# Cosformer attention and a mixture of adapters: the order of numerators, transposition and copy in a slot, q turned further ahead, rows of k retimed

## The chip, the cores and the metric

The kernel runs on one core of a Trainium2 chip. The metric is the device time of one execution in microseconds. Engines are named as in the profile: PE is TensorE, PEld its weight loads, DVE is VectorE, ACT is ScalarE, POOL is GpSimd, SP is SyncE.

## What is computed

Eight batches of eight heads, 576 tokens, head width 64. A linear attention with cosine and sine weights feeds a mixture of eight low-rank adapters, of which each token takes two.

```python
r = np.maximum(x, 0.0)                       # phi, for q and for k
phi = np.concatenate([r * cos_w, r * sin_w], axis=-1)
kv = np.einsum('bhsf,bhsd->bhfd', k_p, v)
z = np.sum(k_p, axis=2)
num = np.einsum('bhsf,bhfd->bhsd', q_p, kv)
den = np.einsum('bhsf,bhf->bhs', q_p, z)[..., None] + 1e-06
x = (num / den)                              # as (4608, 512): token by 8 heads of 64
logits = x @ w_gate                          # 8 adapters, the two largest are kept
w = softmax of the two kept logits
out = x + sum over the two of w * ((x @ A[e]) @ B[e])      # rank 16
```

## The kernel before

The 4608 tokens are 36 tiles of 128. Tiles 0 to 3 are tokens of batch 0, tile 4 holds 64 tokens of batch 0 and 64 of batch 1 (a mixed tile), tiles 5 to 8 are batch 1, tiles 9 to 12 batch 2, 13 is mixed, and so on: two batches take nine tiles, and batch b first appears in tile b // 2 * 9 + b % 2 * 4. The products of k and v of a batch (72 small matmuls, `kv`, in nine rows s of eight) must be done, and copied to SBUF by `kv_out`, before the batch's first tile has its numerators.

The body is one written-out loop over slots n = 0 to 34, one for each tile but the last. `tc.manual_schedule()` leaves each engine's instructions in the order in which the code issues them, so the text of the loop is the order of each engine's queue. What a tile goes through:

- `move_q(n)`: TensorE multiplies q with diagonal matrices of cosines and sines (`transp_q`, line 213, and 201 from tile 27 on), which turns q and weights it; ScalarE empties the two PSUM buffers with a relu (`evac_q`, line 229).
- `numden(n)`: numerators and denominators, eight products into the PSUM tile `nd`, of which there is one (line 257). The epsilon is added by two small products (line 252), or, where `eps_dve(n)` holds (n over 13 and slot n has rows of k), by VectorE (line 268).
- `normalise(n)`: VectorE takes the reciprocal (line 270) and multiplies (line 277) out of `nd` into `xt`.
- `transp_x(n)`: four transpositions on TensorE into `xz` (line 285); `evac_x(n)`, VectorE's copy to `xT` (line 291), which in every third slot takes along the transposed gates of a group (`transp_z`, line 359).
- `logits(n)`: four products (line 311) with the adapters' A and the gate weights. Three tiles form a group.
- `gate_a(g)`, `gate_sig(g)`, `gate_b(g)`: the two largest logits (lines 320 to 328, VectorE), a sigmoid (ScalarE, line 337), and the weighting (lines 344 and 346, VectorE) in the slot after.
- `delta`, `delta_add`, `evac_o`, `store`: the output product or products, ScalarE's copy, for late tiles GpSimd's addition of x, and the DMA to memory. Stores are held back until the loads are through.

k of a batch is turned into its weighted rows by several engines: VectorE clears the negatives of the rows that GpSimd takes (`relu_k`, line 165), GpSimd multiplies these with cosine and sine (`scale_k1`, line 156), VectorE and ScalarE take some rows whole (lines 153 and 151). In which slot, the tables `relu_at`, `pool_at`, `act_at`, `dve_at` and `kv_at` say; they are filled for b = 2 to 7 from `at`, `n_pool` and the batch's first tile. Behind GpSimd's rows of batch b its queue issues the loads of k of b + 3, q of b + 2 and v of b + 3. The gates stand in slots 6, 8, 10, 12, 15, 18, 21, 24, 27, 30 and 33 (`gate_a_at`); from slot 12 on the last logits of the group stand in the same slot, ahead of the gate.

The order of one slot before, on the engines that matter: copy of x of tile n - 1 (DVE), `normalise(n)` (DVE), `move_q(n + 1)` (PE, ACT), rows of k (PE), logits (PE), gates (DVE), output products (PE), `transp_x(n)` and `transp_z` (PE), rows of k (DVE, POOL), `numden(n + 1)` (PE).

Of the kernel before, what the change touches and what calls it, by code (L numbers as in the profile page):

```python
# [13 lines left out]
NS = 9  # L14
# [5 lines left out]
def kernel(ctx, tc, q, k, v, w_gate, A, Bw, out):  # L20
    nc = tc.nc
    B, H, S, D = q.shape
# [8 lines left out]
    NT = B * NS // 2  # L31
# [1 line left out]

    persist = ctx.enter_context(tc.tile_pool(name="persist", bufs=1))
    p_kp = ctx.enter_context(tc.tile_pool(name="p_kp", bufs=3))
    p_qpt = ctx.enter_context(tc.tile_pool(name="p_qpt", bufs=6))
    p_kv = ctx.enter_context(tc.tile_pool(name="p_kv", bufs=3))
    p_x = ctx.enter_context(tc.tile_pool(name="p_x", bufs=14))
    p_xt = ctx.enter_context(tc.tile_pool(name="p_xt", bufs=7))
# [24 lines left out]
    def load_k(b, eng=None):  # L64
        load(eng or nc.gpsimd, k_b[b].rearrange("p g s d -> p g (s d)"), k, b)

    def load_q(b):
        load(nc.gpsimd, q_b[b].rearrange("p g s d -> p g (s d)"), q, b)

    def load_v(b):  # L70
        load(nc.gpsimd, v_b[b][:, 0:VN].rearrange("p (g x) -> p g x", g=G), v, b)
# [161 lines left out]
    def move_q(n):  # L233
        transp_q(n)
        evac_q(n, 0)
        evac_q(n, 1)
# [58 lines left out]
    groups = [list(range(i, i + 3)) for i in range(0, NT - 3, 3)]  # L295
# [130 lines left out]
    def put(at, step, what):  # L426
        at.setdefault(step, []).append(what)
# [5 lines left out]
    kv_at[3] = [(1, s) for s in (5, 4, 7, 8, 6)]  # L433
    for b in range(2, B):
        first = b // 2 * NS + b % 2 * 4
        at = {2: 5, 3: 8, 4: 12, 5: 17, 6: 20, 7: 23}[b]
        n_pool = {2: 5, 3: 7, 4: 8, 5: 8}.get(b, 9)
        for s0, s1 in ((0, 3), (3, n_pool)):
            put(relu_at, at, (b, s0, s1))
        for s in range(n_pool):  # L440
            put(pool_at, at, (b, s))
        for i in range(2):
            if n_pool <= 7:
                put(dve_at, at, (b, 7, i))
            if n_pool < 9:
                put(act_at, first - 4 + i, (b, 8, i))
            if n_pool == 5:
                put(act_at, first - 3 + i, (b, 6, i))
                put(act_at, first - 2, (b, 5, i))
        order = (7, 0, 1, 2, 3, 4, 8, 6, 5) if n_pool <= 7 else (0, 1, 2, 3, 4, 5, 8, 6, 7)  # L450
        if n_pool == 9:
            order = range(NS)
        for j, s in enumerate(order):

            if b == 2:
                ahead = 2 if j < 4 else 1
            elif b == 3:
                ahead = 3 if j < 2 else 2 if j < 5 else 1
            else:
                ahead = 4 - min(j // 2, 3)  # L460
            put(kv_at, first - ahead, (b, s))

# [15 lines left out]
    with tc.manual_schedule():  # L480
# [17 lines left out]
        load_q(2)  # L498
        load_k(3)
        load_v(3)  # L500
        load_k(4)
        load_q(3)
        load_v(4)
        kv_out(0)
        transp_q(0)
        evac_q(0, 0, "dve")
        evac_q(0, 1)
        numden(0)

        g10, g11, g12 = range(len(groups) - 3, len(groups))  # L510
        todo, held = [], []
# [11 lines left out]
                held.append(d)  # L523

        for n in range(NT - 1):
            if n > 0:
                g = move_at.get(n - 1, (None,))[0]
                evac_x(n - 1, g)
                if g is not None:
                    todo += groups[g]  # L530
            normalise(n)
            if n != 3:
                move_q(n + 1)
            for b, s in kv_at.get(n, ()):
                kv(b, s)
                if kv_n[b] == NS:
                    kv_out(b)
            for t in early_at.get(n, ()):
                logits(t)
            if n == 3:  # L540
                move_q(n + 1)
            for g in gate_a_at.get(n, ()):
                gate_a(g)
            for g in gate_b_at.get(n, ()):
                gate_b(g)
            now = todo[:2 if len(todo) > 3 and n not in kv_at else 1]
            del todo[:len(now)]
            for d in now:
                emit(d, n not in kv_at, add=n > 27)
            for g in gate_a_at.get(n, ()):  # L550
                gate_sig(g)
            transp_x(n)
            for g in move_at.get(n, ()):
                transp_z(g)
            for b, s, i in dve_at.get(n, ()):
                scale_k1(b, s, i, "dve")
            for b, s0, s1 in relu_at.get(n, ()):
                relu_k(b, s0, s1)
            for b, s in pool_at.get(n, ()):
                scale_k(b, s)  # L560
                if (b, s) == pool_at[n][-1]:
                    if b + 3 < B:
                        load_k(b + 3)
                    if b + 2 < B:
                        load_q(b + 2)
                    if b + 3 < B:
                        load_v(b + 3)
                    if b + 3 == B - 1:

                        nc.sync.dma_start(out=first_loads, in_=k_b[B - 1][0:1, 0, 0, 0:8])  # L570
                        for d in held:
                            store(d)
                        held = None
            for t in late_at.get(n, ()):
                logits(t)
            numden(n + 1)
            for b, s, i in act_at.get(n, ()):
                scale_k1(b, s, i, "act")

# [56 lines left out]
```

## Time and profile before

| | |
|---|---|
| median of 3 runs | 114.40 us (114.26 to 114.58) |
| the profiled execution | 114.54 us, span 112.8 us, granted clock 0.996 |
| busy in the span | PE 96.1, DVE 83.7, ACT 78.2, POOL 72.3 us |
| stretch 13.3 to 40.7 us (slots 0 to about 10) | PE busy 22.79 of 27.40 us |
| stretch 40.7 to 69.5 us (slots 11 to 21) | PE busy 28.30 of 28.80 us |
| stretch 69.5 to 93.2 us (slots 22 to 31) | PE busy 22.63 of 23.70 us |

A line of the timeline has start and duration in us, engine, source line, operation, tiles written and read, shapes and count; brackets at its end give the engine's idle time before it and what ended that. A line of the chain of waits that ended last has start, duration and what. The end of a matmul is modelled. Span and execution differ by what lies around the instructions, 1.74 us here.

### The profile page before, as it was taken

What the parts mean: (1) busy time and instruction counts of PE and PEld (TensorE: products, weight loads), DVE (VectorE), ACT (ScalarE), POOL (GpSimd) and SP (SyncE); (2) the same over time, 40 slices, a digit from 0 to 9 for tenths busy, and PEclk for the clock granted to TensorE, in tenths of its full rate; (3) what the DMA queues carried; (4) which work ended last, traced back from release to release, by engine and by line L of the source; (5) the groups of instructions that cost most, each with busy time, mean ns of one, the idle gap of its engine ahead of it and who ended that gap; (6) DMA issues with size and microseconds to landing.
All of it is one profiled execution on the core that took longest, in us unless ns stands there. A gap on an engine that the chain in (4) does not pass through costs nothing.

```text
span 112.8 us, 4956 instructions
## 1 busy us (share of the span) xinstructions
PE 96.1 (85%) x2050; PEld 74.1 (66%) x2068; DVE 83.7 (74%) x296; ACT 78.2 (69%) x169; POOL 72.3 (64%) x134
## 2 busy tenths in 40 slices
PE   2999676978899899999999999998998997978710
PEld 1347465867796788868788888785786886754200
DVE  5598489459969677695987998999949589786620
ACT  5087579755986595797876978856777777895720
POOL 5992223228995996299939999989980445774000
PEclk9999999999999999999999999999999999999998
DMA  2999999999999999999999999999999424526892
GB/s 41 385 206 208 213 202 210 210 180 208 208 208 209 207 209 209 209 206 213 204 207 208 208 209 208 242 348 383 381 324 366 142 100 97 185 101 226 285 340 82
DMA packets 19670, 24.77 MB, mean 220 GB/s; under 512 B 2624, under 2 KB 14528, under 8 KB 19648
## 3 DMA queue, kind: packets, MB, share of 16 engines
q0 software_dynamic: 13856, 13.84, 73.8%
q1 hardware_dynamic: 5792, 10.62, 26.9%
q8 instruction: 16, 0.26, 0.9%
q14 instruction: 6, 0.05, 0.1%
HBM read 28.85 MB, written 9.44 MB: 340 GB/s over the span
## 4 chain that ended last, share of the span: by engine, by line
PE 40%; DMA 28%; DVE 15%; issue 4%; POOL 4%; ACT 4%; POOLq 0%; DVEq 0%; ACTq 0%
DMA k<-in_k_dram 14%; DMA v<-in_v_dram 12%; PE cd L180 9%; PE za L311 7%; PE qd L213 6%; PE xz L285 5%; PE nd L257 4%; DVE xt L277 4%; PE dx L377 3%; DVE k L165 3%; DVE xT L291 2%; DVE zg L346 2%; ACT osb L408 2%; PE qd L201 2%; DMA out_dram<-osb 2%
## 5 line engine op out<-in xcount | busy, mean ns | idle before, releaser
L229 ACT ACTIVATE qpT<-qd 128x512 bf16<-128x512 f32 x71 | 38.6, 595 | 15.0 <-PE qd L213 10.9
L156 POOL TENSOR_SCALAR kp<-k,cos_tab 128x256 bf16<-128x256 bf16 x46 | 22.6, 490 | 7.1 <-DVE k L165 6.5
L277 DVE TENSOR_TENSOR xt<-nd,rden 128x512 bf16<-128x512 f32 x36 | 24.9, 691 | 1.3
L291 DVE COPY xT<-xz 128x512 bf16<-128x512 bf16 (+1 forms) x36 | 17.1, 476 | 9.9 <-PE xz L359 6.4
L156 POOL TENSOR_SCALAR kp<-k,sin_tab 128x256 bf16<-128x256 bf16 x46 | 21.9, 476 | 0.0
L180 PE MATMUL cd<-v,kp 64*128 64x128 bf16 x576 | 20.3, 217 | 0.9 <-DVE kp L153 0.9
L285 PEld LDWEIGHTS <-xt 128*128 128x128 bf16 x144 | 10.8, 115 | 12.1 <-DVE xt L277 7.9
L285 PE MATMUL xz<-ident,xt 128*128 128x128 bf16 x144 | 14.4, 222 | 5.0 <-DVE xt L277 4.3
L180 PEld LDWEIGHTS <-kp 64*128 64x128 bf16 x576 | 16.3, 94 | 3.1 <-issue 0.9
L257 PE MATMUL nd<-kvsb,qpT 128*128 128x65 bf16 (+1 forms) x320 | 16.7, 195 | 1.1 <-DVE qpT L231 0.5
L213 PE MATMUL qd<-diag,q 128*64 128x128 bf16 x432 | 17.3, 222 | 0.3 <-DMA q<-in_q_dram 0.3
L402 POOL TENSOR_TENSOR osb<-osb,xt 128x512 f32<-128x512 f32 x8 | 9.2, 1160 | 9.6 <-ACT osb L408 8.0
L408 ACT COPY osb<-dx 128x512 f32<-128x512 f32 x19 | 11.2, 588 | 5.9 <-remote 2.1
L213 PEld LDWEIGHTS <-q 128*64 128x64 bf16 x432 | 13.1, 109 | 1.8 <-DMA q<-in_q_dram 0.5
L257 PEld LDWEIGHTS <-qpT 128*128 128x128 bf16 (+1 forms) x320 | 12.7, 100 | 1.9 <-ACT qpT L229 0.7
L311 PE MATMUL za<-AW,xT 128*128 128x144 bf16 x140 | 12.4, 227 | 0.7 <-DVE zg L346 0.5
L311 PEld LDWEIGHTS <-xT 128*128 128x128 bf16 x144 | 9.0, 98 | 3.2 <-DVE xT L291 1.0
L408 ACT COPY osb<-cd 128x512 f32<-128x512 f32 x16 | 9.1, 597 | 1.3 <-PE cd L382 1.3
L62 POOL DMA_DIRECT2D v<-in_v_dram x8 | 6.2, 778 | 5.2 <-DMA q<-in_q_dram 4.4
L485 PE MATMUL wu<-wide,ones 128*128 128x512 bf16 x24 | 7.3, 477 | 2.0 <-DVE AW L115 2.0
L62 POOL DMA_DIRECT2D q<-in_q_dram x8 | 6.1, 763 | 3.6 <-DMA k<-in_k_dram 3.6
L62 POOL DMA_DIRECT2D k<-in_k_dram x7 | 5.4, 771 | 3.9 <-DMA k<-in_k_dram 2.2
(75 smaller groups left out, 133.8 us busy)
## 6 DMA issues: line engine op xcount, KB each, us to landing
out_dram<-osb SPq DMA_DIRECT2D x32, 256.0 KB, 3.9
v<-in_v_dram POOLq DMA_DIRECT2D x8, 576.0 KB, 16.5
q<-in_q_dram POOLq DMA_DIRECT2D x8, 576.0 KB, 15.6
k<-in_k_dram POOLq DMA_DIRECT2D x7, 576.0 KB, 15.5
k0f<-in_k_dram SPq DMA_DIRECT2D x1, 1152.0 KB, 5.4
out_dram<-osb SPq DMA_DIRECT2D x8, 128.0 KB, 2.4
AW<-in_moe_A_dram POOLq DMA_DIRECT2D x1, 128.0 KB, 18.2
Ball<-in_moe_B_dram POOLq DMA_DIRECT2D x1, 128.0 KB, 16.7
```

What stands on the lines that cost most here:

```text
L62: eng.dma_start(out=t, in_=rows(dram, b))
L156: nc.gpsimd.tensor_scalar(out=dst, in0=src, scalar1=tab, scalar2=1.0, op0=ALU.mult, op1=ALU.mult)
L180: nc.tensor.matmul(out=kvz[par][:, g], lhsT=kp_t[b][pr, s, g], rhs=v_rhs(b, g, s, pr), start=(first and g == 0), stop=(last and g == G - 1))
L213: nc.tensor.matmul(out=t[cols, j, 2 * gi:2 * gi + 2, :], lhsT=q_b[b][:, 2 * gp + gi, s, :], rhs=diag[:, s, i], start=(j == 0 and gi == 0), ...
L229: nc.scalar.activation(t, src, AF.Relu)
L257: nc.tensor.matmul(out=nd[pr, gg, j * W:(j + 1) * W], lhsT=qpT[:, j, pr], rhs=kv_t[b][:, h % 2, h // 2, :], start=(eps_dve(n) and j == 0), ...
L277: nc.vector.tensor_tensor(out=x, in0=nd[:, :, :, 0:D], in1=rden.rearrange("p (g j) -> p g j", g=2).to_broadcast([128, 2, 4, D]), op=ALU.mult)
L285: nc.tensor.transpose(out=xz[:, c * 128:(c + 1) * 128], in_=x[:, c], identity=ident)
L291: nc.vector.tensor_copy(t[:, 0:c], xz[:, 0:c * 128].rearrange("p (c s) -> p c s", c=c))
L311: nc.tensor.matmul(out=za_t[g][:, i, :], lhsT=xT[:, c, :], rhs=AW[:, :, c, :], start=(c == 0 and i == 0), stop=(c == DCH - 1), skip_group_ ...
L402: nc.gpsimd.tensor_tensor(out=t, in0=t, in1=xt_t.pop(n), op=ALU.add)
L408: nc.scalar.copy(t, src)
```

## The change

In a slot n whose next tile does not begin a batch (n + 1 is not in the new list `late`: 4, 9, 13, 18, 22, 27, 31, 35), `numden(n + 1)` comes right behind `normalise(n)`, and `transp_x(n)` with `transp_z` behind it, ahead of the rows of k. Where n + 1 is in `late`, both keep their places late in the slot. The copy of tile n - 1's x comes behind `normalise(n)`; where n is in `late` it stays ahead of it. q of tile m is turned in slot m - 2 for the first tiles and most others up to 17, in slot m - 3 from tile 18 on, in slot m - 1 for tiles 4, 9 and 13; tiles 5, 10 and 14 are turned at the end of slot m - 2. Tile 1's q is turned ahead of the loop, and the pool of turned q has eight buffers instead of six. The slots in which k is cleared and weighted move (2: 5 to 6, 3: 8 to 10, 4: 12 to 14, 6: 20 to 21, 7: 23 to 25), a few rows go from GpSimd to ScalarE (one of batch 3, one of batch 6), and the products of k and v of batches 3, 4 and 5 are spread otherwise, so that slots 10, 14 and 18 have none. The load of q of batch 3 goes ahead of k of batch 4.

```diff
@@ -33,7 +33,7 @@
 
     persist = ctx.enter_context(tc.tile_pool(name="persist", bufs=1))
     p_kp = ctx.enter_context(tc.tile_pool(name="p_kp", bufs=3))
-    p_qpt = ctx.enter_context(tc.tile_pool(name="p_qpt", bufs=6))
+    p_qpt = ctx.enter_context(tc.tile_pool(name="p_qpt", bufs=8))
     p_kv = ctx.enter_context(tc.tile_pool(name="p_kv", bufs=3))
     p_x = ctx.enter_context(tc.tile_pool(name="p_x", bufs=14))
     p_xt = ctx.enter_context(tc.tile_pool(name="p_xt", bufs=7))
@@ -433,8 +433,8 @@
     kv_at[3] = [(1, s) for s in (5, 4, 7, 8, 6)]
     for b in range(2, B):
         first = b // 2 * NS + b % 2 * 4
-        at = {2: 5, 3: 8, 4: 12, 5: 17, 6: 20, 7: 23}[b]
-        n_pool = {2: 5, 3: 7, 4: 8, 5: 8}.get(b, 9)
+        at = {2: 6, 3: 10, 4: 14, 5: 17, 6: 21, 7: 25}[b]
+        n_pool = {2: 5, 3: 6, 4: 8, 5: 8, 6: 8}.get(b, 9)
         for s0, s1 in ((0, 3), (3, n_pool)):
             put(relu_at, at, (b, s0, s1))
         for s in range(n_pool):
@@ -443,22 +443,40 @@
             if n_pool <= 7:
                 put(dve_at, at, (b, 7, i))
             if n_pool < 9:
-                put(act_at, first - 4 + i, (b, 8, i))
+                put(act_at, first - 3 if b < 4 else first - 4 + i, (b, 8, i))
+            if n_pool <= 6:
+                put(act_at, first - 2, (b, 6, i))
             if n_pool == 5:
-                put(act_at, first - 3 + i, (b, 6, i))
-                put(act_at, first - 2, (b, 5, i))
+                put(act_at, first - 3 + i, (b, 5, i))
         order = (7, 0, 1, 2, 3, 4, 8, 6, 5) if n_pool <= 7 else (0, 1, 2, 3, 4, 5, 8, 6, 7)
         if n_pool == 9:
             order = range(NS)
         for j, s in enumerate(order):
 
-            if b == 2:
+            if b < 4:
                 ahead = 2 if j < 4 else 1
-            elif b == 3:
+            elif b < 6:
                 ahead = 3 if j < 2 else 2 if j < 5 else 1
             else:
                 ahead = 4 - min(j // 2, 3)
             put(kv_at, first - ahead, (b, s))
+
+
+
+    late = [b // 2 * NS + b % 2 * 4 for b in range(1, B)] + [NT - 1]
+    q_at, q_end = {}, {}
+    for m in range(2, NT):
+        first = max(f for f in [0] + late[:-1] if f <= m)
+        if first == 0:
+            put(q_at, m - 2, m)
+        elif first > 13:
+            put(q_at, m - 3, m)
+        elif m == first:
+            put(q_at, m - 1, m)
+        elif m == first + 1:
+            put(q_end, m - 2, m)
+        else:
+            put(q_at, m - 2, m)
 
 
 
@@ -498,14 +516,15 @@
         load_q(2)
         load_k(3)
         load_v(3)
+        load_q(3)
         load_k(4)
-        load_q(3)
         load_v(4)
         kv_out(0)
         transp_q(0)
         evac_q(0, 0, "dve")
         evac_q(0, 1)
         numden(0)
+        move_q(1)
 
         g10, g11, g12 = range(len(groups) - 3, len(groups))
         todo, held = [], []
@@ -523,14 +542,28 @@
                 held.append(d)
 
         for n in range(NT - 1):
-            if n > 0:
+            def evac_before():
                 g = move_at.get(n - 1, (None,))[0]
                 evac_x(n - 1, g)
-                if g is not None:
-                    todo += groups[g]
+                return groups[g] if g is not None else []
+
+            if n > 0 and n in late:
+                todo += evac_before()
             normalise(n)
-            if n != 3:
-                move_q(n + 1)
+            if n + 1 not in late:
+                numden(n + 1)
+            if n > 0 and n not in late:
+                todo += evac_before()
+            for m in q_at.get(n, ()):
+                if m == n + 2:
+                    move_q(m)
+            if n + 1 not in late:
+                transp_x(n)
+                for g in move_at.get(n, ()):
+                    transp_z(g)
+            for m in q_at.get(n, ()):
+                if m != n + 2 and n != 3:
+                    move_q(m)
             for b, s in kv_at.get(n, ()):
                 kv(b, s)
                 if kv_n[b] == NS:
@@ -549,9 +582,10 @@
                 emit(d, n not in kv_at, add=n > 27)
             for g in gate_a_at.get(n, ()):
                 gate_sig(g)
-            transp_x(n)
-            for g in move_at.get(n, ()):
-                transp_z(g)
+            if n + 1 in late:
+                transp_x(n)
+                for g in move_at.get(n, ()):
+                    transp_z(g)
             for b, s, i in dve_at.get(n, ()):
                 scale_k1(b, s, i, "dve")
             for b, s0, s1 in relu_at.get(n, ()):
@@ -573,7 +607,10 @@
                         held = None
             for t in late_at.get(n, ()):
                 logits(t)
-            numden(n + 1)
+            if n + 1 in late:
+                numden(n + 1)
+            for m in q_end.get(n, ()):
+                move_q(m)
             for b, s, i in act_at.get(n, ()):
                 scale_k1(b, s, i, "act")
 
```

## The prediction

> **What bounds the kernel now.** I read the page first, then the busy time by stretch, then the timeline of single slots. NORM(n), ND(n), TX(n), TZ(g), LG(n) and DX(n) stand for the normalisation, numerators, transposition, transposed gates, logits and output products of tile n or group g.
>
> ```profile
> span 112.8 us, 4956 instructions
> PE 96.1 (85%) x2050; PEld 74.1 (66%) x2068; DVE 83.7 (74%) x296; ACT 78.2 (69%) x169; POOL 72.3 (64%) x134
> PEclk9999999999999999999999999999999999999998
> 13.30:40.70 27.40, 22.79 (x535) 19.37 (x535) 20.81 (x72) 19.83 (x45) 16.73 (x31) 1.00 1.27 205
> 40.70:69.50 28.80, 28.30 (x598) 23.13 (x604) 23.02 (x76) 22.37 (x49) 23.87 (x48) 1.00 1.21 208
> 51.92:101.26 49.34, 46.50 (x1128) 37.79 (x1138) 41.56 (x138) 38.19 (x82) 37.48 (x69) 1.00 0.92 231
> ```
>
> In a stretch row the columns are length, then busy time of PE, PEld, DVE, ACT and POOL, then clock and DMA. From 40.7 us TensorE is the bound: 28.30 of 28.80 us busy. From ND(15) at 51.92 to ND(35) at 101.26 at most 2.84 us are idle. So there the change can win little, and every wait that it adds before a product lengthens the run. Only the first stretch has something to win: 4.6 us idle.
>
> The profiled execution took 114.54 us, 1.74 outside its span; it lies 0.14 above the median, 114.40. I sum against 114.54.
>
> **The gate slots.** This is slot 15 to 16 of before:
>
> ```profile
> 53.39 0.42 PE L311 MATMUL za<-AW,xT 128*128 128x144 bf16 x4
> 53.65 0.38 PE L377 MATMUL dx<-xt,ident 128*128 128x512 bf16 x1
> 53.85 0.32 DVE L320 MAX8 m<-za 128x8 f32<-128x8 f32 x3
> 54.08 0.39 PE L285 MATMUL xz<-ident,xt 128*128 128x128 bf16 x4
> 54.30 0.41 PE L257 MATMUL nd<-kvsb,qpT 128*128 128x65 bf16 x8
> 54.40 0.18 DVE L328 SCALAR_TENSOR_TENSOR tg<-za,nm 128x24 f32<-128x24 f32 x1
> 54.50 0.42 DVE L291 COPY xT<-xz 128x512 bf16<-128x512 bf16 x1
> 54.84 0.15 DVE L268 TENSOR_SCALAR den<-nd 128x8 f32<-128x8 f32 x1
> 55.27 0.69 DVE L277 TENSOR_TENSOR xt<-nd,rden 128x512 bf16<-128x512 f32 x1
> ```
>
> The gate (MAX8 to tg) waits for the logits, which end at 53.81, and starts 0.04 later; it takes 0.73. Copy and NORM(16) queue behind it on VectorE, NORM taking 1.12 (54.84 to 55.96). Before, this chain had a whole slot: TX(15) and ND(16) follow on TensorE at once, since they need only NORM(15), and TX(16) comes two microseconds later.
>
> After, ND(17) is the first product of slot 16. The nd buffer is single, so it waits for NORM(16), and NORM(16) still queues behind the gate of slot 15. The q turns, TX and rows of k that could fill the time are queued behind ND(17) on TensorE. It may start 0.04 + 0.73 − 0.08 (VectorE starts its next instruction that much early, as at 54.50) + 1.12 + 0.06 = 1.87 us after the logits' end. TensorE has only DX(7), and is free at 54.08, 0.27 after. That is 1.6 us of new idle time, in slots 15, 24 and 27; in slot 18 a second output (0.43, from 53.65 to 54.08) leaves 1.2. **Together 6.0 us.** The 0.06 is seen where before already meets such a wait (gate 10):
>
> ```profile
> 99.57 0.69 DVE L277 TENSOR_TENSOR xt<-nd,rden 128x512 bf16<-128x512 f32 x1
> 100.32 0.41 PE L285 MATMUL xz<-ident,xt 128*128 128x128 bf16 x4 [0.39 <-DVE xt L277]
> ```
>
> **The change of batch.** At the end of slots 17, 21, 26 and 30 the order stays TX, TZ, ND, but the next slot now opens with another ND, which wants copy and NORM first. Before, 16 products of q, rows of k, logits and an output lay between. Slot 17 to 18 of before prices the chain:
>
> ```profile
> 59.48 0.33 PE L359 MATMUL xz<-ident,zg 128*128 128x128 bf16 x3
> 59.64 0.41 PE L257 MATMUL nd<-kvsb,qpT 128*128 128x65 bf16 x8
> 59.84 0.62 DVE L291 COPY xT<-xz 128x896 bf16<-128x896 bf16 x1 [0.94 <-PE xz L359]
> 59.98 0.64 PE L213 MATMUL qd<-diag,q 128*64 128x128 bf16 x16
> 60.81 0.69 DVE L277 TENSOR_TENSOR xt<-nd,rden 128x512 bf16<-128x512 f32 x1
> ```
>
> TZ ends at 59.81, NORM at 61.50; with 0.06 the next ND may start at 61.56, while TensorE is free at 59.98. At slot 26 to 27 that is 1.6 us of idle time. Tile 18 has no rows of k in its slot any more, so its epsilon moves from VectorE (0.19) to TensorE (0.07): 1.3. **2.9 us.**
>
> Slots 21 and 30 have both a gate and a batch change. For these I need a mixed tile's ND, 46.67 to 47.28, and the clearing of k's negatives:
>
> ```profile
> 46.67 0.17 PE L252 MATMUL nd<-eps_hi,ones 128*128 128x4 bf16 x1
> 47.28 0.61 PE L213 MATMUL qd<-diag,q 128*64 128x128 bf16 x16
> 58.15 0.75 DVE L165 TENSOR_SCALAR k<-k 128x768 bf16<-128x768 bf16 x2
> 73.57 2.36 DVE L165 TENSOR_SCALAR k<-k 128x768 bf16<-128x768 bf16 x2
> ```
>
> Slot 21: gate 0.77, clearing 0.75, copy 0.42, NORM without its epsilon 0.93, less three overlaps of 0.08, plus 0.06, is 2.7 after the logits; TensorE has output 0.27, TX 0.22 and ND(22) 0.61: idle 1.6. Slot 30 without the clearing: 2.0 against 0.88, idle 1.1. **2.7 us.** Slot 33 to 34: 0.77 − 0.08 + 0.93 + 0.06 = 1.7 against three single products of 0.21 (0.48 after the logits): idle 1.2, of which 0.39 was there: **0.8 us.**
>
> The clearing took 2.36 us beside GpSimd's rows of batch 6 and 0.75 with GpSimd idle. [...]
>
> **q two or three slots ahead.** The q products are the same. In slot 15 alone two tiles' q stand with one TX (0.22) between them, and the two qd buffers must be emptied first:
>
> ```profile
> 55.28 1.07 ACT L229 ACTIVATE qpT<-qd 128x512 bf16<-128x512 f32 x2
> ```
>
> An eviction pair takes 1.07, behind a row of k8 on ScalarE: the wait is between 0 and 0.9, taken 0.7, since little but that TX stands in between. Where NORM comes behind copy and the gate's second half, a light slot may wait 0.25, twice. **1.2 us** (0 to 2). Elsewhere an early q costs nothing: its eviction hides under the rows of k, which it did before too.
>
> **The first fourteen slots.** Before loses time here at most TX (the first row, from the waits, gives total, times and longest):
>
> ```profile
> PE xz L285 <- DVE xt L277: 4.3, 10, 0.6
> 4.62 13.85 DMA v<-in_v_dram
> 14.41 0.41 PE L285 MATMUL xz<-ident,xt 128*128 128x128 bf16 x4 [0.46 <-DVE xt L277]
> 18.52 1.07 PE L180 MATMUL cd<-v,kp 64*128 64x128 bf16 x32 [0.91 <-DVE kp L153]
> 21.48 0.65 ACT L188 CAST kvsb<-cd 128x260 bf16<-128x260 f32 x2 [0.66 <-PE cd L180]
> 27.25 0.48 POOL L156 TENSOR_SCALAR kp<-k,cos_tab 128x256 bf16<-128x256 bf16 x1 [0.45 <-DVE k L165]
> 31.36 0.47 POOL L156 TENSOR_SCALAR kp<-k,sin_tab 128x256 bf16<-128x256 bf16 x1
> 34.42 0.29 DVE L153 TENSOR_SCALAR kp<-k,cos_tab 128x256 bf16<-128x256 bf16 x1 [0.21 <-DMA k<-in_k_dram]
> 34.82 0.69 DVE L165 TENSOR_SCALAR k<-k 128x768 bf16<-128x768 bf16 x2
> 35.28 0.58 POOL L156 TENSOR_SCALAR kp<-k,cos_tab 128x256 bf16<-128x256 bf16 x1 [1.21 <-DVE k L165]
> 41.30 0.48 POOL L156 TENSOR_SCALAR kp<-k,sin_tab 128x256 bf16<-128x256 bf16 x1
> 44.59 1.07 PE L180 MATMUL cd<-v,kp 64*128 64x128 bf16 x32
> ```
>
> That 0.46 is the time of NORM, and ND now waits for it in TX's place, so the cycle NORM, ND, NORM keeps its length; moreover batch 1's products cannot start before its v lands at 18.47. Up to slot 6 I count no gain.
>
> Then the retimed rows cost. Batch 2's clearing now stands in slot 6 behind NORM and gate 0, so GpSimd starts at about 30.8 instead of 27.25: a slot of 2.5 later (the mean of the twenty in 49.34 us), with 0.73 for the gate and 0.3 for its logits. Its ten instructions take 4.6 us (27.25 to 31.83), to 35.4, and the products of the last four rows follow them (0.27 each, as 32 take 1.07): 36.7. The eviction of kv (0.65) and ND(9) reach to 38.0, NORM(9) to 39.1; ND(10), q, TX, an output and three logits to 41.5; gate 2 (0.73), two rows of k (34.42 to 34.82) and clearing (0.69) put GpSimd's start for batch 3 at 43.4. Twelve instructions of 0.46 take it to 48.9; before, fourteen ended at 41.78. Two rows' products later batch 3 is done, near 49.6 instead of 45.66. **4.0 us late** into the dense part. From below: the new order wins back its waits and nothing is lost (0); from above: each k tile is also waited for singly (6). I take 4, since chain and rows give it. The loads have reserve, being issued on GpSimd behind these rows but several transfers ahead.
>
> **Gained back:** the idle time that the 2.36 us clearing caused, and some of the 2.84 us: 1.3.
>
> **Sum:** 6.0 + 2.9 + 2.7 + 0.8 + 1.2 + 4.0 − 1.3 = 16.3; 114.5 + 16.3 = 130.8, said as **131 us**.
>
> **Rivals.**
> *Faster.* Place: slots 0 to 10. ND ahead takes NORM off TensorE's path, the 4.6 us idle before 40.7 vanish, and the 1.3 with them: 114.5 − 5.9 = 108.6. For it: before waits there at nearly every TX. Against it: v at 18.47, and the gate chain. It decides if all the new waits together stay under 5.9 us, that is, if the gates find their logits a slot earlier than the order says. Chance 0.06.
> *Half.* The early part comes out even, and batch changes find a filler; only the gate slots wait: 6.0 + 2.7 = 8.7, so 123. Chance 0.17.
> *Clock.* With an idle time in most slots the granted clock falls. The slowest group of 128x512 products here, the warm-up, took 477 ns against 380:
>
> ```profile
> L485 PE MATMUL wu<-wide,ones 128*128 128x512 bf16 x24 | 7.3, 477 | 2.0 <-DVE AW L115 2.0
> ```
>
> A quarter more on 46.50 busy us is 12 us: 143. Against it: the clock row shows 9 throughout and 1.00 from 13.3 to 40.7, with 4.6 of 27.4 us idle. [...] Chance 0.03.
> *No change:* gains and waits cancel. Chance 0.01.
>
> **How the numbers follow.** Forecast 0.73, at 131. Range 121 to 136: down to the half case with a smaller gate wait, up to early costs of 6 and a port contention; it leaves out the faster case and the clock, and the tails. A measurement of this kernel can tell about 0.3%. Faster 0.06, same 0.01, slower 0.93.
>
> **What would show it.** Right: ND's products (L257) wait for DVE xt, about 1.6 us each time, in slots after a gate, and the waits of PE for xt grow from 4.3 us to over 12; TensorE's dense stretch shows holes every third slot; GpSimd's second block of k rows starts near 31, its third near 43. Wrong: the gates' MAX8 starts before the logits of its own slot, or ND starts while VectorE still normalises, or no idle time stands ahead of ND.

## The result and the profile after

| | before | after |
|---|---|---|
| median (lowest to highest) | 114.42 us (114.26 to 114.58) | 136.56 us (134.06 to 140.71) |
| profiled execution | 114.54 | 134.06 |
| its span, mean granted clock | 112.8, 0.996 | 132.3, 0.990 |

The ratio is 1.177 [1.168, 1.186]. It compares the executions of after at a clock of 0.986 and 0.990; two others ran at 0.956 and 0.934 and took 137.84 and 140.71, which is why the median stands higher than 1.177 times 114.42. The profiled execution, against which the sum was made, rose by 19.5 us; 16.3 was predicted.

The page of after: the span, busy times, the row of TensorE's busy tenths and the clock row.

```profile
span 132.3 us, 4962 instructions
PE 99.5 (75%) x2053; PEld 73.7 (56%) x2072; DVE 81.1 (61%) x294; ACT 80.3 (61%) x173; POOL 70.0 (53%) x130
PE   3997788696889798984896698596685598586830
PEclk9999999999999999999999999999999999999996
```

VectorE's and GpSimd's busy times fell and ScalarE's rose by 2.1, yet the span grew by 19.5. TensorE is idle for 132.3 − 99.5 = 32.8 us, where it was 112.8 − 96.1 = 16.7: 16.1 of the 19.5. Slices of 5 to 7 tenths recur to the end of the busy row. The clock row is full but for its last slice, and there the clock fell when TensorE had finished (129.7 us, its last product at 127.1), so this execution owes nothing to the clock. The other 3.4 us are TensorE's own busy time.

One reservation: the page counts 2072 weight loads but 2053 products. On every other line the two are equal in number (576 and 576 on L180, 432 and 432 on L213); the 19 records that are missing, and 18 before (2050 of 2068), are all of output products (lines 377, 382 and 397). So TensorE's idle time, as its records give it, is somewhat too long on both sides. If each missing product is put 0.21 us behind its neighbour with a length of 0.38, the rhythm of the recorded ones, busy time becomes about 97.6 and 101.6 us (an estimate), and the difference between the kernels hardly changes.

The stretches of after; the third runs from ND(15) to ND(35), the fourth from NORM(14) to NORM(34):

```profile
13.70:43.60 29.90, 24.43 (x542) 19.63 (x543) 20.24 (x71) 19.84 (x44) 11.23 (x19) 1.00 1.27 206
43.60:80.00 36.40, 29.24 (x582) 22.36 (x588) 21.66 (x71) 24.46 (x54) 25.59 (x51) 1.00 1.10 203
55.20:120.77 65.57, 49.04 (x1158) 38.55 (x1171) 39.39 (x139) 40.68 (x86) 40.86 (x77) 1.00 0.64 162
53.90:118.80 64.90, 49.35 (x1166) 38.70 (x1175) 38.76 (x137) 40.87 (x86) 38.89 (x75) 1.00 0.66 162
```

From ND(15) to ND(35) before took 49.34 us with 2.84 idle; after takes 65.57 with 16.5 idle. By NORM the same part took 49.4 before (50.2 to 99.6) and takes 64.9: 15.5 of the 19.5 us arise there, 3.7 ahead of NORM(14), 0.3 behind NORM(34).

The waits of after (total, times, longest):

```profile
DVE m L320 <- PE za L311: 22.9, 11, 3.7
PE nd L257 <- DVE xt L277: 10.1, 7, 1.6
PE nd L252 <- DVE xt L277: 6.0, 9, 1.3
POOL kp L156 <- DVE k L165: 18.4, 5, 5.7
PE qd L201 <- ACT osb L408: 1.1, 2, 0.5
PE qd L213 <- ACT osb L408: 0.7, 2, 0.3
```

Numerators now wait 16.1 us for the normalisation (L257 and L252, the same products with an epsilon ahead), where the transposition waited 4.3. The first row is the other half of the loop: VectorE sits idle for 22.9 us until logits come, and TensorE then sits idle until VectorE has worked through gate and normalisation. Slot 15 to 16 of after:

```profile
60.58 0.42 PE L311 MATMUL za<-AW,xT 128*128 128x144 bf16 x4
60.84 0.38 PE L377 MATMUL dx<-xt,ident 128*128 128x512 bf16 x1
61.04 0.32 DVE L320 MAX8 m<-za 128x8 f32<-128x8 f32 x3 [3.69 <-PE za L311]
61.59 0.18 DVE L328 SCALAR_TENSOR_TENSOR tg<-za,nm 128x24 f32<-128x24 f32 x1
61.69 0.15 DVE L268 TENSOR_SCALAR den<-nd 128x8 f32<-128x8 f32 x1
62.12 0.69 DVE L277 TENSOR_TENSOR xt<-nd,rden 128x512 bf16<-128x512 f32 x1
62.72 0.41 DVE L291 COPY xT<-xz 128x512 bf16<-128x512 bf16 x1
62.86 0.41 PE L257 MATMUL nd<-kvsb,qpT 128*128 128x65 bf16 x8 [1.64 <-DVE xt L277]
```

The logits end at 61.00, the gate starts 0.04 later, NORM(16) ends at 62.81, ND(17) starts 0.05 later: 1.86 behind the logits, where 1.87 was predicted. Less the 0.27 after which the prediction has TensorE free, that is 1.59 against 1.6. The 1.64 at the end of the row comes so near by accident: the output's second product (line 382) is one of the missing records, and with it the gap that the profile shows would be about 1.4. The batch change 17 to 18 in the same timeline:

```profile
68.64 0.33 PE L359 MATMUL xz<-ident,zg 128*128 128x128 bf16 x3
69.01 0.62 DVE L291 COPY xT<-xz 128x896 bf16<-128x896 bf16 x1 [3.16 <-PE xz L359]
69.78 0.69 DVE L277 TENSOR_TENSOR xt<-nd,rden 128x512 bf16<-128x512 f32 x1
70.53 0.42 PE L257 MATMUL nd<-kvsb,qpT 128*128 128x65 bf16 x8 [1.26 <-DVE xt L277]
```

And the start of the second and the third block of k rows:

```profile
30.92 0.56 DVE L165 TENSOR_SCALAR k<-k 128x768 bf16<-128x768 bf16 x2
31.47 0.47 POOL L156 TENSOR_SCALAR kp<-k,cos_tab 128x256 bf16<-128x256 bf16 x1 [4.28 <-DVE k L165]
43.50 0.62 DVE L165 TENSOR_SCALAR k<-k 128x768 bf16<-128x768 bf16 x2
43.95 0.51 POOL L156 TENSOR_SCALAR kp<-k,cos_tab 128x256 bf16<-128x256 bf16 x1 [5.70 <-DVE k L165]
```

One wait was not in the sum. In slot 17 q's products find the two buffers that they share with the outputs still full, because ScalarE copies an output (osb) first:

```profile
65.39 0.41 PE L213 MATMUL qd<-diag,q 128*64 128x128 bf16 x8
65.49 0.58 ACT L408 COPY osb<-dx 128x512 f32<-128x512 f32 x1 [0.39 <-PE qd L213]
66.13 0.41 PE L213 MATMUL qd<-diag,q 128*64 128x128 bf16 x8 [0.33 <-ACT osb L408]
```

### The profile page after: what moved, and what is told of

It is laid out like the page before. It is cut to its first block, busy times and chain, and to the rows that moved or that the text cites. A ratio compares the mean times of both kernels' runs of the same rounds, so it can differ in the third digit from the quotient of the medians.

```text
span 132.3 us, 4962 instructions
## 1 busy us (share of the span) xinstructions
PE 99.5 (75%) x2053; PEld 73.7 (56%) x2072; DVE 81.1 (61%) x294; ACT 80.3 (61%) x173; POOL 70.0 (53%) x130
## 4 chain that ended last, share of the span: by engine, by line
PE 45%; DVE 19%; ACT 14%; DMA 7%; issue 6%; POOL 5%; another core or an unknown queue 1%; POOLq 0%; ACTq 0%; DVEq 0%
PE qd L213 9%; PE cd L180 8%; ACT qpT L229 8%; PE za L311 7%; DMA q<-in_q_dram 7%; PE nd L257 6%; DVE xt L277 6%; PE xz L285 5%; POOL kp L156 4%; PE qd L201 4%; ACT osb L408 3%; DVE m L320 2%; ACT kp L151 2%; PE cd L382 2%; DVE xT L291 2%
## 5 line engine op out<-in xcount | busy, mean ns | idle before, releaser
L156 POOL TENSOR_SCALAR kp<-k,cos_tab 128x256 bf16<-128x256 bf16 x44 | 21.2, 482 | 27.7 <-DVE k L165 18.4
L257 PE MATMUL nd<-kvsb,qpT 128*128 128x65 bf16 (+1 forms) x320 | 17.4, 195 | 12.0 <-DVE xt L277 10.1
L257 PEld LDWEIGHTS <-qpT 128*128 128x128 bf16 (+1 forms) x320 | 12.8, 100 | 16.4 <-DVE xt L277 6.5
L180 PE MATMUL cd<-v,kp 64*128 64x128 bf16 x576 | 20.5, 217 | 0.8 <-POOL kp L156 0.4
L156 POOL TENSOR_SCALAR kp<-k,sin_tab 128x256 bf16<-128x256 bf16 x44 | 20.7, 470 | 0.0
L213 PE MATMUL qd<-diag,q 128*64 128x128 bf16 x432 | 17.8, 222 | 1.7 <-ACT osb L408 0.7
L180 PEld LDWEIGHTS <-kp 64*128 64x128 bf16 x576 | 16.1, 94 | 3.6 <-ACT kp L151 1.1
L320 DVE MAX8 m<-za 128x8 f32<-128x8 f32 x35 | 3.8, 162 | 22.9 <-PE za L311 22.9
L213 PEld LDWEIGHTS <-q 128*64 128x64 bf16 x432 | 13.2, 110 | 4.4 <-issue 2.3
L402 POOL TENSOR_TENSOR osb<-osb,xt 128x512 f32<-128x512 f32 x8 | 9.1, 1156 | 10.5 <-ACT osb L408 10.5
L408 ACT COPY osb<-dx 128x512 f32<-128x512 f32 x16 | 9.4, 588 | 6.4 <-remote 3.5
L285 PEld LDWEIGHTS <-xt 128*128 128x128 bf16 x144 | 10.3, 115 | 4.7 <-DVE xt L277 2.2
L311 PE MATMUL za<-AW,xT 128*128 128x144 bf16 x140 | 12.4, 227 | 0.4 <-DVE zg L346 0.3
L252 PE MATMUL nd<-eps_hi,ones 128*128 128x4 bf16 x44 | 7.3, 173 | 6.3 <-DVE xt L277 6.0
L408 ACT COPY osb<-cd 128x512 f32<-128x512 f32 x19 | 10.8, 593 | 2.0 <-PE cd L382 1.8
## 6 DMA issues: line engine op xcount, KB each, us to landing
Ball<-in_moe_B_dram POOLq DMA_DIRECT2D x1, 128.0 KB, 16.7
```

The costliest lines, as they stand in the source:

```text
L156: nc.gpsimd.tensor_scalar(out=dst, in0=src, scalar1=tab, scalar2=1.0, op0=ALU.mult, op1=ALU.mult)
L180: nc.tensor.matmul(out=kvz[par][:, g], lhsT=kp_t[b][pr, s, g], rhs=v_rhs(b, g, s, pr), start=(first and g == 0), stop=(last and g == G - 1))
L213: nc.tensor.matmul(out=t[cols, j, 2 * gi:2 * gi + 2, :], lhsT=q_b[b][:, 2 * gp + gi, s, :], rhs=diag[:, s, i], start=(j == 0 and gi == 0), ...
L257: nc.tensor.matmul(out=nd[pr, gg, j * W:(j + 1) * W], lhsT=qpT[:, j, pr], rhs=kv_t[b][:, h % 2, h // 2, :], start=(eps_dve(n) and j == 0), ...
L285: nc.tensor.transpose(out=xz[:, c * 128:(c + 1) * 128], in_=x[:, c], identity=ident)
L311: nc.tensor.matmul(out=za_t[g][:, i, :], lhsT=xT[:, c, :], rhs=AW[:, :, c, :], start=(c == 0 and i == 0), stop=(c == DCH - 1), skip_group_ ...
```

## The experiments

The theory: the order of each slot puts ND behind a VectorE chain whose head, the gate, waits for logits of the same slot. The main rivals: the late rows of k, the early q, and the granted clock. Ratios are to before, with 95% intervals; "idle in the dense part" is TensorE's idle time between NORM(14) and NORM(34), summed over the gaps between its products by the product that ends each gap (before 2.2 us; after 15.6, of which 11.65 ahead of ND, 2.7 ahead of q, 1.1 ahead of outputs). With the missing records filled in as above it would be about 1.1 and 13.7, and ND's part 10.5. The two doubled kernels, the one with earlier logits and the last one have all their records; the others lack 18 or 19.

**The three parts one by one.** First the rows of k alone, in the kernel before:

```
-        at = {2: 5, 3: 8, 4: 12, 5: 17, 6: 20, 7: 23}[b]
+        at = {2: 6, 3: 10, 4: 14, 5: 17, 6: 21, 7: 25}[b]
...  (and the other row tables of the change)
```

> The kernel before with only the rows of k retimed and shared out as in the change; order of the slots and turning of q as before. Theory (the rows of batches 2 and 3 start one and two slots later on GpSimd, and their products wait for them singly, 4.8 us of such waits with this order in the run with the order of before): 118 to 120, with the idle time of TensorE ahead of kv products in slots 7, 8, 11 and 12. Rival 1 (the rows are hidden, and only the new order or the early q makes them visible): 114.5. Rival 2 (a lower granted clock in these stretches adds to it): over 121, with half-clock time over 6 us in the trace.

Measured 121.03 us, 1.053 [1.047, 1.060], which is 6.1 us on 114.4, above the 4.0 of the sum. Its waits show TensorE waiting for single rows of k, which before did not:

```profile
PE cd L180 <- POOL kp L156: 3.6, 7, 0.7
```

And its stretches in the profiled execution (121.89) show the clock halved behind each of the two places (the clock is the third number from the right):

```profile
30.40:33.80 3.40, 1.72 (x38) 1.14 (x33) 1.62 (x6) 2.57 (x7) 3.40 (x8) 1.00 1.21 208
33.80:37.20 3.40, 3.40 (x52) 3.14 (x51) 1.92 (x9) 0.97 (x2) 3.21 (x6) 0.50 1.21 211
44.00:47.40 3.40, 1.80 (x44) 1.19 (x44) 2.66 (x8) 2.03 (x6) 2.89 (x7) 1.00 1.21 208
47.40:50.80 3.40, 3.18 (x33) 2.56 (x36) 0.43 (x2) 1.39 (x3) 3.40 (x8) 0.50 1.21 209
```

So chain and clock both have a share: the time lies just over 121 with 6.8 us at half clock, which are the signs of Rival 2, and the single waits of the theory are there too. 16 of q's products took 1.06 us in the first of the two (35.49 in its timeline), against 0.64 in before (59.98). By the 0.50 of the rows, 3.4 us at half clock put off at most 1.7 us of work (an estimate), twice; two other executions, at a clock of 0.984 instead of 0.967, took 120.1 and 120.2.

Then q alone, in the kernel before: the change's `q_at` and `q_end`, with what belongs to them (tile 1's q ahead of the loop, eight buffers, the load of q of batch 3 ahead of k of batch 4), and the slot's order and the rows as before.

```
-            if n != 3:
-                move_q(n + 1)
+            for m in q_at.get(n, ()):
+                if m == n + 2:
+                    move_q(m)
+            for m in q_at.get(n, ()):
+                if m != n + 2 and n != 3:
+                    move_q(m)
...
+            for m in q_end.get(n, ()):
+                move_q(m)
```

> The kernel before with only q turned ahead as in the change; order of the slots and rows of k as before. Theory: where two tiles' q stand back to back, the second waits for ScalarE to empty the two PSUM buffers, 3.0 us in the first fourteen slots and 1.2 later in the run with the order of before: 117 to 118.5. Rival (the prediction's: an early q costs nothing where its eviction hides): 114.5 to 115.

Measured 118.52, 1.035 [1.032, 1.038]: an early q by itself costs 4.0 us, as expected. The row that is new in its waits:

```profile
PE qd L213 <- ACT qpT L229: 2.6, 5, 0.5
```

q's products arrive before ScalarE has emptied their two buffers, mostly in the first fourteen slots: NORM(14) starts at 53.0 instead of 50.2, and the dense part takes 51.1 us instead of 49.4.

Then all of the change but the order within a slot (q early, rows late, TX ahead of ND as before):

```
-            if n + 1 not in late:
-                numden(n + 1)
...
-            if n + 1 in late:
-                transp_x(n)
+            transp_x(n)
...
-            if n + 1 in late:
-                numden(n + 1)
+            numden(n + 1)
```

> The changed kernel with the order of before in each slot (copy, normalisation, q, rows of k, logits, gate, outputs, transposition, numerators); q still two or three slots ahead and the rows of k still retimed. Theory: the waits of numerators behind gates and at changes of batch (12 us) and of q behind an output (2 us) go, the late rows stay (4.4): 118 to 120. Rival 1 (rows): 128 or more. Rival 2 (nothing but the order costs): 114.5.

Measured 126.52 (124.36 to 127.53; 1.105 by the medians, without an interval). Three of its four executions had a mean clock of 0.956 to 0.969; the fourth, at 0.983, took 124.36. Its dense part as a stretch:

```profile
60.30:111.80 51.50, 47.65 (x1144) 38.67 (x1151) 39.20 (x136) 39.14 (x84) 39.77 (x76) 1.00 0.73 189
```

And the two rows of its waits that stand for late rows and early q:

```profile
PE cd L180 <- POOL kp L156: 3.7, 6, 1.0
PE qd L213 <- ACT qpT L229: 2.6, 5, 0.5
```

The dense part is back at 51.5 us, so the order is what lengthened it. But the start is worse than after's: NORM(14) at 60.3 against 53.9. The expectation of 118 to 120 missed by 4.4 us at least, because it let the costs of after stand for those of the parts. Under the old order the late rows and the early q hit TensorE at full price, and in the profiled execution the clock was halved for 10.2 us ahead of NORM(14) (32.2 to 39.0 and 49.2 to 52.6), which by the same estimate puts off at most 5.1 us of work. Under the new order TensorE waits for single rows of k for only 0.4 us in all. That fits ND's waits giving GpSimd and ScalarE the time that they lack, but no run separates it from the clock.

The reverse, the whole change with the old row tables:

```
-        at = {2: 6, 3: 10, 4: 14, 5: 17, 6: 21, 7: 25}[b]
+        at = {2: 5, 3: 8, 4: 12, 5: 17, 6: 20, 7: 23}[b]
...  (and the other row tables of before)
```

> The changed kernel with the tables of the rows of k (slots, engines, spread) of the kernel before. Theory: the first fourteen slots get back what the late rows cost, 4.4 us (batch 3's last products at 50.0 instead of 45.7), so 129 to 131; the gate and batch waits stay. Rival 1 (the late rows cost most of the loss): 120 or less. Rival 2 (the early slots are set by the cycle of normalisation and numerators, and the rows are hidden): 134.

Measured 132.78, 1.156 [1.151, 1.162]; above the 129 to 131 expected. NORM(14) comes 2.3 us earlier than in after, and the row of ND in its waits stays:

```profile
PE nd L257 <- DVE xt L277: 10.4, 7, 1.6
```

So in the new order the late rows cost about (1.177 − 1.156) × 114.4 = 2.4 us, not 6.1, and the order on top of an early q costs (1.156 − 1.035) × 114.4 = 13.8. The parts do not add: rows and q cost 6.1 and 4.0 alone, and part of the 6.1 is clock.

**The gate chain.** If gate and ND meet on VectorE, the gate behind the next normalisation frees ND:

```
             for g in gate_a_at.get(n, ()):
-                gate_a(g)
...
             if n > 0 and n not in late:
                 todo += evac_before()
+            for g in gate_a_at.get(n - 1, ()):
+                gate_a(g)
+                gate_sig(g)
```

> The changed kernel, but the first half of each gate and its sigmoid stand in the next slot, behind that slot's normalisation and copy. Theory (numerators wait for a normalisation that queues behind the gate): the idle times of 1.64 us ahead of the numerators in slots 16, 25 and 28 and the 1.0 in 19 go, and part of those in 13, 22, 31 and 34: 6 to 9 us of the changed kernel's 134.1, so 125 to 128. Rival 1 (the late rows of k cost the time): no change, 134. Rival 2 (the granted clock): no change of the time beyond what the clock of the run shows.

Measured 131.57, 1.139 [1.132, 1.146]: about half of what was expected. The waits of the gate slots are gone (ND(17) follows an output without a wait), and ND's row in its waits fell:

```profile
PE nd L257 <- DVE xt L277: 5.9, 6, 1.5
```

But this is slot 20 to 21 in its timeline:

```profile
71.95 0.56 DVE L346 TENSOR_TENSOR zg<-za,em 128x384 bf16<-128x384 f32 x1
72.85 0.69 DVE L277 TENSOR_TENSOR xt<-nd,rden 128x512 bf16<-128x512 f32 x1
73.60 0.40 PE L257 MATMUL nd<-kvsb,qpT 128*128 128x65 bf16 x8 [0.74 <-DVE xt L277]
```

In the slot behind a gate the gate's second half (zg) now stands ahead of NORM(20), and ND(21) waits 0.74 for that. In this order the gate is a load on VectorE that an early ND meets in another slot.

The other end of the chain: logits earlier, ahead of q and rows of k, so that the gate can start sooner.

```
+            for t in early_at.get(n, ()):
+                logits(t)
             for m in q_at.get(n, ()):
                 if m != n + 2 and n != 3:
                     move_q(m)
...
-            for t in early_at.get(n, ()):
-                logits(t)
             if n == 3:
```

> The changed kernel, but the logits of a slot stand on TensorE ahead of the early q and the rows of k instead of behind them; nothing else moves. Theory (the numerators of the next slot wait for a normalisation that queues behind the gate, and the gate waits for the slot's last logits): the gate now starts earlier by what stood ahead of the logits (q 0.57 and rows of k 0.55 to 1.1), so the waits of 1.64 us ahead of ND fall to 0.5 or less in slots 15, 24 and 27, that of slot 21 by 1, those after pure batch changes stay: 5 to 7 us less, 127 to 129. Rival (the waits come from ND's place alone, whatever the gate does): 134.

Measured 130.53, 1.140 [1.135, 1.145]. Two rows of its waits:

```profile
PE nd L257 <- DVE xt L277: 4.5, 6, 1.4
PE za L311 <- DVE xT L291: 1.2, 2, 0.9
```

ND's idle time in the dense part fell from 11.65 (10.5 with the missing records) to 5.9, and 1.2 came back as logits that wait for their copy. The time between logits and ND is what sets the wait, as the theory says; the whole was 1.5 us slower than the slowest expected.

The cost itself, doubled: the first half of each of the thirteen gates (MAX8 to tg, 0.73 us) is computed twice, in both kernels.

```
     def gate_a(g):
+        gate_a1(g)
+        gate_a1(g)
```

> The changed kernel with every first half of a gate computed twice on VectorE (0.73 us more in each of eleven slots; the result is the same). Theory: it stands whole between logits and numerators, and shows in nearly every gate slot: 5 to 7 us more, 139 to 141. Rival (the waits ahead of ND come from elsewhere, VectorE being busy 61% of the span): under 2 us more, 134 to 136.

> The kernel before with every first half of a gate computed twice. Theory: the same 0.73 has 0.2 to 0.4 us of reserve in the dense slots, since TensorE has a slot of work before it needs the normalisation behind the gate: 3 to 4 us more, 117.5 to 118.5, a third to a half less than in the changed kernel. Rival 1 (no reserve here either, so that the order did not spend one): as much as in the changed kernel, over 119.5. Rival 2 (full cover): 115 or less.

Before rose by 4.2 us, to 118.69, 1.037 [1.035, 1.039]; after to 145.29, 1.255 [1.251, 1.259], which is (1.255 − 1.177) × 114.4 = 8.9. Logits and ND of slot 15 to 16 in the doubled after:

```profile
62.60 0.42 PE L311 MATMUL za<-AW,xT 128*128 128x144 bf16 x4
65.52 0.40 PE L257 MATMUL nd<-kvsb,qpT 128*128 128x65 bf16 x8 [2.06 <-DVE xt L277]
```

And TX's row in the waits of the doubled before, where the same chain ends on TX:

```profile
PE xz L285 <- DVE xt L277: 5.7, 11, 1.0
```

In the doubled after ND(17) starts 2.50 behind the end of the logits instead of 1.86, and by the same 0.64 later in slots 18, 21, 24 and 27: the second copy of the gate shows whole. Summed over the eleven gate slots, the distance from the last logits to the next ND grows by 6.0 us, within the 5 to 7 expected. The rest of the 8.9 goes along with the clock, which the expectation left out: the two executions that the ratio takes had a mean clock of 0.941 and 0.952, those of after 0.990 and 0.986, and the profiled one (148.0 us, a span of 146.2) had 0.916, which comes to about 2 × (1 − 0.916) × 146.2 = 24.6 us at half clock, the end of the span included (an estimate). So by the chain the new order pays about 6 us for the longer gate where the old one pays 4.2. That it is twice as sensitive is not shown.

**q behind the rows of k** in slots 17, 21, 26 and 30, of after:

```
+            q_late = n in (17, 21, 26, 30)
             for m in q_at.get(n, ()):
-                if m != n + 2 and n != 3:
+                if m != n + 2 and n != 3 and not q_late:
                     move_q(m)
             for b, s in kv_at.get(n, ()):
...
+            for m in q_at.get(n, ()):
+                if q_late:
+                    move_q(m)
```

> The changed kernel, but in slots 17, 21, 26 and 30 the rows of k stand ahead of the turned q. Theory: there q opens the slot right behind an output product that sits in the same two PSUM buffers, and waits for ScalarE to empty it, about 0.5 us each time; with the rows of k ahead the wait is covered: 2 us less, 132. Rival (q ahead costs nothing, as the prediction had it): 134. Rival 2: the wait only moves to the rows of k or to ND at the end of the slot, 134.

Measured 134.05, 1.168 [1.165, 1.172]. The waits of L213 and L201 for osb are gone and the dense idle time ahead of q falls from 2.7 to 0.5; that ahead of outputs rises from 1.1 to 2.3, for they wait in turn for q's eviction. The intervals of this kernel and of after overlap, so a gain is not resolved.

**All repairs together** (gate behind, q behind the rows, q ahead of ND where a batch begins, rows of before):

```
+            if n in (18, 22, 27, 31):
+                for m in q_at.pop(n):
+                    move_q(m)
             if n + 1 not in late:
                 numden(n + 1)
...  (with the three edits above)
```

> The changed kernel with four things undone or covered at once: gates behind the next normalisation, rows of k ahead of q in slots 17, 21, 26 and 30, q ahead of the numerators in slots 18, 22, 27 and 31, rows of k as before. Theory: of the 11.7 us of waits ahead of ND in slots 14 to 34 about 3 are left (batch changes, where q covers 0.6 of each 1.3 to 1.6, and slots 19 and 28 behind gate and sigmoid), of the 2.7 ahead of q 1; the late rows' 2 us go: 134.1 less 12 to 13, 121 to 123. Rival 1 (waits only move to the next instruction): 127 or more. Rival 2 (the new order itself is sound and only the gates hurt): 115 to 117.

Measured 128.95, 1.123 [1.117, 1.128]. That is nearer to the rival, that waits only move, than to the theory: TensorE still stands idle 8.2 us ahead of ND in the dense part, the longest times 1.80 (slot 32), 1.20 (slot 23) and 1.03 (the batch change 26 to 27), and 0.74 in slot 20, where after has no such wait.

**Towards something faster.** The wait that before does have, the clearing of 2.36 us beside GpSimd, goes with one retimed block:

```
-        at = {2: 5, 3: 8, 4: 12, 5: 17, 6: 20, 7: 23}[b]
+        at = {2: 5, 3: 8, 4: 12, 5: 17, 6: 20, 7: 25}[b]
```

> The kernel before with one number changed: the rows of batch 7 are cleared and weighted in slot 25 instead of 23. Theory: the clearing that takes 2.36 us beside GpSimd's rows of batch 6 takes about 0.8 with GpSimd idle, and TensorE's waits that follow it (0.40 ahead of xz, 0.16 ahead of za) go: 113.9 to 114.1. Rival 1 (that idle time is given back later, at the end of the loads or at the outputs): 114.5. Rival 2 (batch 7's products or GpSimd's additions of the last tiles come too late): over 114.8.

Measured 113.96 over 12 runs, 0.9949 [0.9933, 0.9964]: 0.6 us faster than before, the only kernel here that beats both. TensorE's idle time in the dense part falls with it, from 2.2 to 1.7 us. The clearing's line in the kernel before (minimum, median and maximum ns of one instruction):

```profile
L165 DVE TENSOR_SCALAR k<-k x12: 275/453/1899, 26.6 to 75.4; 128x768 bf16<-128x768 bf16 x6, 128x1280 bf16<-128x1280 bf16 x2, 128x1536 bf16<-128x1536 bf16 x2, 128x512 bf16<-128x512 bf16 x1
```

The slowest of these ends at 75.47, 0.2 us behind the last of GpSimd's rows of batch 6 (75.26). The same line with this edit, where the slowest takes half as long:

```profile
L165 DVE TENSOR_SCALAR k<-k x12: 284/384/959, 27.5 to 80.3; 128x768 bf16<-128x768 bf16 x6, 128x1280 bf16<-128x1280 bf16 x2, 128x1536 bf16<-128x1536 bf16 x2, 128x512 bf16<-128x512 bf16 x1
```

On top of it, gate 10 behind NORM(34), against the 0.39 wait that the prediction quoted:

```
+            if n == NT - 2:
+                gate_a(g10)
+                gate_sig(g10)
...  (and slot 33 leaves its gate out)
```

> The kernel before with the rows of batch 7 in slot 25, and gate 10 behind the normalisation of slot 34 instead of ahead of it in slot 33. Theory: the wait of 0.39 us ahead of the transposition of tile 34 goes, and the output of the last tiles is not later for it: 113.5. Rival (the gate's second half and the transposed gates of group 10 come later by as much): 114.0, the time of the version with batch 7's rows alone, or above.

Measured 115.04, 1.008 [1.005, 1.011]: 1.3% worse than without it. The 0.39 did not go (0.36 at 99.73 of its timeline), and in its timeline the logits next in order wait behind the whole gate:

```profile
101.40 0.66 PE L311 MATMUL za<-AW,xT 128*128 128x144 bf16 x4 [1.26 <-DVE zg L346]
```

This profiled execution (115.94) had a mean clock of 0.973, and four logits took 0.66 us at 101.40 where 0.42 stands at 97.12; the ones at a clock of 0.987 and above took 114.8 to 115.0, so the loss does not come from the clock.

## Why the prediction was right, and where its steps were off

By the ratio the change gives 1.177 × 114.4 = 134.6; the forecast was 131 in 121 to 136. The median of after, 136.56, lies 0.6 above that range. The port contention that the range's upper end counts is shown by no run: the traces show one clearing of 2.36 us, in before, while GpSimd worked on rows of batch 6, and none above 0.82 in after. Direction, bound and mechanism held: VectorE's chain sets ND. The sum came near partly because misses of both signs met in it: the order's terms were 1.0 too high, the early q about 2 too low, and TensorE's own busy time was not in it.

- **Gate slots, 6.0.** 1.64 at slots 15, 24 and 27 and 1.00 at 18: 5.9. The chain from logits to ND is 1.86 long in all four.
- **Batch changes, 2.9.** 1.26 and 1.50: 2.8.
- **Slots 21 and 30, 2.7.** 1.40 and 1.03: 2.4. For slot 30 the sum left out TX (0.22), which does stand between the logits and ND there.
- **Slot 33 to 34, 0.8.** The wait of TX(34) rose from 0.39 to 0.72: 0.3. The third output product ahead of it waits another 0.39, for ScalarE's copy, which the sum did not have. The order's four terms give 11.4 of the 12.4 forecast; another 0.44 ahead of ND, in slot 32, was not foreseen.
- **Late k rows, 4.0.** GpSimd starts at 31.47 and 43.95 where 30.8 and 43.4 stood, batch 3 is done at 50.03 (49.6), 4.4 late, and NORM(14) comes 3.7 late. As the start of the dense part that is right, but as the price of the rows it is luck in part: with the old rows in the new order NORM(14) still comes at 51.6, 1.4 later than before, so 2.3 of the 3.7 are the rows and 1.4 the order and the early q, for which the sum has no term in these slots. Alone the rows cost 6.1, just above the upper bound of 6, and there the clock had joined in.
- **Early q, 1.2: the mis-sized term.** The dense idle time ahead of q rose by 2.55 and that ahead of outputs by 0.8. Slot 15 has about 0.5 of it, where 0.7 stood; 2.2 stand in slots 17, 21, 26 and 30, where nothing was counted. The step that failed is "Elsewhere an early q costs nothing: its eviction hides under the rows of k": it weighed the eviction but not the two buffers, which q shares with outputs and which ScalarE empties in its own order. q alone, 4.0, refutes that sentence for the order before as well.
- **Gained back, 1.3.** No clearing took longer than 0.82 us; GpSimd was idle at the start of each. The dense waits of TX, 1.4 by the records, fell to 0.2. But most of the 1.4 stands where an output product's record is missing, about 0.3 being left with these filled in, so the term is not confirmed by it; moving the slow clearing alone gained 0.6.
- **Left out: TensorE's own busy time,** 99.5 against 96.1. Four epsilon products moved to it, at 0.17 each, account for 0.7 at most. The missing records, 18 and 19, do not explain it either. In slot 15 of after the output starts 0.16 us ahead of the logits' end (60.84 against 61.00), while ND(17) starts behind a wait and overlaps with nothing ahead of it. That the rest is lost overlap of this kind is a guess: no run separates it, and it stays open.

Of the rivals, *faster* failed by its own point of decision: the new waits came to over 11 us, not under 5.9, because the gates found their logits where the order says (0.04 behind). *Half* supposed that batch changes find a filler; they waited 1.26 and 1.50. *Clock* did not decide the profiled execution, at 1.00 through the stretches; in the others it did take part: 0.956 and 0.934 went along with 137.84 and 140.71 us, against 135.27 at 0.986. That idle time in most slots lowers the clock is not shown as a rule, for after itself had between 0.934 and 0.990. Its chance of 0.03 was for a fall throughout; a partial fall belonged in the upper end of the range.

## What to carry to other kernels

Before moving a product ahead, follow its operand back through the queue of the engine that makes it, up to the first instruction that waits for something of the same slot: that distance, less the work that still stands between, is the new wait, and in the gate slots here it came out to a tenth of a microsecond. Before, numerators and gate had a slot's distance between them; with that taken away, the repairs at either end of the chain gained 4 us of 20, and all together 6, for they left or made waits at other slots. Before an idle time is read off a profile, compare the number of products with that of their weight loads: here 18 or 19 products were missing, some of them inside the gaps. Price the parts of a change in its own surroundings: rows of k cost 6.1 us alone, clock included, and 2.4 within it.

## What the runs showed of the hardware

In the traces of before and of after the granted clock is 1.0 until TensorE has finished and 0.5 at the end of the span: the last product ends at 107.6 us in before and at 127.1 in after, and the clock falls at 111.9 and 129.7. In other kernels it fell within the loop, to 0.50, for 3.4 us or twice that. In the two falls quoted for the rows of k TensorE had been busy 1.72 and 1.80 of the 3.40 us before, and no single wait of its products between 30 and 52 us was over 0.7. The same in two stretches of after with the old rows, where the gaps are those of a gate slot (no wait over 1.6 in the loop):

```profile
89.40:92.80 3.40, 1.65 (x61) 1.43 (x60) 3.19 (x14) 1.30 (x5) 3.40 (x8) 1.00 0.32 117
92.80:99.60 6.80, 5.65 (x81) 4.40 (x82) 0.86 (x3) 3.44 (x8) 0.20 (x1) 0.50 0.10 39
```

In the doubled after the clock fell at 67.2 us, behind 3.40 us with 1.68 busy, and at 101.3, behind 3.40 with 1.34 busy; no wait in its loop was over 2.1. These two falls start 34.1 us apart, those of the kernel with the rows of k alone (33.8 and 47.4) 13.6. The profiled execution of after holds a half idle stretch and kept its clock (two of its stretches):

```profile
91.50:94.90 3.40, 1.64 (x60) 1.43 (x60) 3.25 (x14) 1.72 (x6) 0.27 (x1) 1.00 0.32 114
94.90:98.30 3.40, 2.63 (x66) 1.93 (x68) 1.22 (x3) 2.63 (x7) 3.40 (x8) 1.00 0.21 77
```

So 1.64 busy of 3.40 was followed by a full clock here and 1.65 by a halved one with the old rows: in this case a half idle stretch did not by itself bring a fall. What else belongs to one is not shown, nor which executions are hit: the kernel with the rows of k alone had a mean clock of 0.967 and 0.968 in two executions and of 0.984 in two.
